# Sorted v re-tiled through DRAM and x^T by crossbar DMA, for the last two batches, with loads and attention alternating

## The chip, the cores and the metric

One core of a Trainium2 chip. The time is the device time of one execution in microseconds (us), each kernel run several times. "Span" is the length of one profiled execution; it leaves out about 2 us that the device time has on top. In the profiles PE is TensorE, PEld its weight loads, DVE VectorE, ACT ScalarE, POOL GpSimd and SP SyncE (SPq its queue); PSUM is the memory that matmuls write to, and a copy out of it frees a slot.

## The reference, cut to what matters

```python
# q, k, v: (4, 8, 768, 64); sort_net: (4, 8, 8, 8); w_in: (512, 2048); w_out: (2048, 512)
P = sinkhorn(sort_net)                                   # five rounds of exp and normalizing
k_sorted = einsum('bhij,bhjcd->bhicd', P, k_blocks)      # 8 blocks of 96 rows, mixed by P
v_sorted = einsum('bhij,bhjcd->bhicd', P, v_blocks)
attn = softmax(q_block @ k_sorted_block.T / 8)           # inside each block of 96 only
x = (attn @ v_sorted_block)  ->  (3072 tokens, 512)
out = relu(x @ w_in)**2 @ w_out                          # the FFN
```

## The kernel before

Everything on TensorE is bf16. Tokens are cut in 8 FFN groups of 384, two to a batch. A group is 28 chunks: 16 up-projections of 4 matmuls (128x384) and 12 quarter down-projections of 4 matmuls (128x512). The attention of a batch is worked off in 4 pairs of heads and slipped between the chunks of earlier groups. A small planner in the Python code simulates the engines with given costs and so fixes the order of all instructions; the chip then runs that order, whatever the true durations are.

For one head pair the sort of v, the transposes that re-tile sorted v by block, and the transposes of x are all on TensorE, each with a copy out of PSUM:

```python
def s_sort(u, t, due=0, ...):            # t = 1: k, t = 2: v
    for a in range(NA):                  # 6
        for h in range(2):               # weights of 64 columns: 12 narrow matmuls
            nc.tensor.matmul(out=tp[64 * h:64 * (h + 1), a, :],
                lhsT=src[:, 2 * u.hp + h, D * a:D * (a + 1)],
                rhs=w_all[:, H * u.b + 2 * u.hp + h, ...], start=True, stop=True)
    ...                                  # cast to ksT or vsT
def s_vt(u, due=0):                      # 8 transposes of vsT, then a copy to vs
    ...
def s_xt(u, due=0):                      # 8 transposes of ao, then a copy to xT
    ...
for b, (c0, c1) in enumerate(((n_up, 2 * n_up), (2 * n_up, 4 * n_up), (4 * n_up, 6 * n_up)), 1):
    lay(b, (0, 1), c0, c1)               # batch 1 beside group 1; 2 beside 2, 3; 3 beside 4, 5
```

PSUM is full: one slot `p1` (q, v and x transposes), two slots `p2` (sorts, scores, attention times v), three for the FFN.

The softmax here doesn't subtract the row's maximum and nothing guards it: scores larger than these inputs give would overflow.

## Time and profile before

| | before |
|---|---|
| time, median of 3 | 241.82 us |
| span of the profiled run | 238.9 us |
| TensorE busy | 96% |
| one FFN group alone | 20.76 us |

TensorE sets the time. The readings are in the prediction below. **The attention of batches 2 and 3 on TensorE's path** is the stretch from the end of batch 1's last FFN chunk to the first up-projection of group 6, less the four FFN groups in it (4 x 20.76 = 83.04 us). Before, the stretch is 193.28 - 85.61 = 107.67 us, so this attention costs 24.6 us.

### The profile page before, as it was taken

How to read it: one execution, taken by the hardware profiler on the slowest of the kernel's cores; microseconds unless marked ns; L12 is line 12 of the kernel's file. 1: busy time of each engine (PE TensorE's matmuls, PEld its weight loads, DVE VectorE, ACT ScalarE, POOL GpSimd, SP SyncE). 2: the span in 40 equal slices, each digit the busy share in tenths (PEclk: the TensorE clock that was granted, in tenths of full speed). 3: DMA queues.
4: the chain of work that ended last, by engine and by line, in shares of the span. 5: the costliest groups of instructions: out<-in, count | busy, mean ns of one | idle time of the engine just before them, and what ended most of it. 6: DMA issues, size and time to landing. Idle time of an engine off the chain costs nothing.

```text
span 238.9 us, 5867 instructions
## 1 busy us (share of the span) xinstructions
PE 230.5 (96%) x2485; PEld 138.1 (58%) x2501; DVE 121.4 (51%) x322; ACT 123.0 (51%) x256; POOL 27.0 (11%) x41
## 2 busy tenths in 40 slices
PE   7899999999999999999999999999999999999993
PEld 2777665556675556655665456655665456446541
DVE  6677777327785347744676037643666025105400
ACT  4365675237885247724674147723674147227510
POOL 8843221500006000000000000000000000000000
PEclk9999999999999999999999999999999999999999
DMA  6999999999405990011100120011100120011012
GB/s 81 193 204 207 206 207 206 201 241 222 76 3 68 220 238 9 3 44 47 45 3 0 44 91 0 3 44 47 44 3 1 47 88 1 19 72 44 0 44 88
DMA packets 20489, 20.30 MB, mean 85 GB/s; under 512 B 1008, under 2 KB 17392, under 8 KB 20464
## 3 DMA queue, kind: packets, MB, share of 16 engines
q0 software_dynamic: 16960, 13.63, 36.8%
q1 hardware_dynamic: 3504, 6.30, 7.2%
q8 instruction: 19, 0.31, 0.5%
q14 instruction: 6, 0.05, 0.1%
HBM read 27.27 MB, written 6.29 MB: 140 GB/s over the span
## 4 chain that ended last, share of the span: by engine, by line
PE 91%; DVE 4%; ACT 2%; issue 1%; POOL 0%; POOLq 0%
PE hp L562 35%; PE op L590 34%; PE tp L403 5%; PE vbp L472 3%; PE qtp L361 3%; PE oup L499 3%; PE scp L439 3%; PE xtp L531 3%; ACT qT L166 1%; DVE p_sb L266 1%; PE fill L283 0%; DVE vs L168 0%; ACT h L570 0%; DVE rs L265 0%; POOL qb L212 0%
## 5 line engine op out<-in xcount | busy, mean ns | idle before, releaser
L562 PE MATMUL hp<-xT,w_in_bf 128*128 128x384 bf16 x512 | 92.8, 326 | 0.0
L590 PE MATMUL op<-w_out_bf,h 128*128 128x512 bf16 x368 | 86.2, 379 | 1.0 <-issue 0.3
L570 ACT ACTIVATE h<-hp 128x384 bf16<-128x384 f32 x128 | 62.3, 494 | 26.1 <-PE hp L562 25.4
L573 DVE TENSOR_TENSOR h<-h 128x384 bf16<-128x384 bf16 x128 | 43.9, 354 | 37.2 <-ACT h L570 36.7
L562 PEld LDWEIGHTS <-w_in_bf 128*128 128x128 bf16 x512 | 46.4, 98 | 28.1
L590 PEld LDWEIGHTS <-h 128*128 128x128 bf16 x384 | 36.1, 98 | 39.7
L166 ACT COPY ob<-op 128x512 f32<-128x512 f32 x24 | 14.1, 586 | 57.5 <-PE op L590 57.5
L455 ACT ACTIVATE et<-scp 96x384 bf16<-96x384 f32 x64 | 26.4, 490 | 6.7 <-PE scp L439 6.7
L509 DVE TENSOR_TENSOR ao<-oup,rec 96x512 bf16<-96x512 f32 x32 | 22.0, 687 | 1.1
L168 DVE COPY vs<-vbp 96x1024 bf16<-96x1024 bf16 (+1 forms) x20 | 11.6, 580 | 19.5 <-PE vbp L472 19.4
L168 DVE COPY qT<-qtp 128x768 bf16<-128x768 bf16 (+1 forms) x15 | 7.3, 489 | 18.9 <-PE qtp L361 18.4
L166 ACT CAST ksT<-tp 128x768 bf16<-128x768 f32 (+1 forms) x17 | 11.7, 686 | 9.9 <-PE tp L403 9.6
L168 DVE COPY xT<-xtp 128x768 bf16<-128x768 bf16 (+1 forms) x16 | 7.9, 496 | 13.3 <-PE xtp L531 12.8
L283 PE MATMUL fill<-ones 128*128 128x128 bf16 (+1 forms) x108 | 12.0, 255 | 1.5 <-DVE ones L185 1.5
L499 PEld LDWEIGHTS <-et 96*128 96x128 bf16 x256 | 10.7, 98 | 3.1 <-ACT h L570 0.6
L168 DVE CAST vsT<-tp 128x768 bf16<-128x768 f32 (+1 forms) x14 | 11.8, 840 | 0.8
L499 PE MATMUL oup<-vs,et 96*128 96x65 bf16 x256 | 11.6, 193 | 0.2 <-DVE vs L168 0.2
L361 PEld LDWEIGHTS <-qb 128*64 128x64 bf16 (+1 forms) x240 | 6.9, 109 | 7.1 <-issue 5.8
L508 DVE RECIPROCAL rec<-oup 96x8 f32<-96x8 f32 x32 | 6.4, 199 | 8.3 <-PE oup L499 8.1
L472 PE MATMUL vbp<-ident,vsT 128*128 128x128 bf16 x128 | 10.5, 219 | 0.0
L212 POOL DMA_DIRECT2D qb<-in_q_dram x8 | 6.0, 747 | 39.1 <-PE qtp L361 33.3
L361 PE MATMUL qtp<-ident,qb 128*64 128x128 bf16 (+1 forms) x240 | 9.3, 212 | 0.8 <-DVE qT L168 0.4
(48 smaller groups left out, 130.5 us busy)
## 6 DMA issues: line engine op xcount, KB each, us to landing
out_dram<-ob SPq DMA_DIRECT2D x24, 256.0 KB, 2.0
qb<-in_q_dram POOLq DMA_DIRECT2D x8, 384.0 KB, 12.4
kb<-in_k_dram POOLq DMA_DIRECT2D x6, 384.0 KB, 15.1
vb<-in_v_dram POOLq DMA_DIRECT2D x6, 384.0 KB, 16.3
w_in_bf<-in_moe_w_in_dram POOLq DMA_DIRECT2D x4, 512.0 KB, 13.2
w_out_bf<-in_moe_w_out_dram POOLq DMA_DIRECT2D x4, 512.0 KB, 19.3
kb<-in_k_dram POOLq DMA_DIRECT2D x4, 192.0 KB, 6.1
vb<-in_v_dram POOLq DMA_DIRECT2D x4, 192.0 KB, 6.4
```

What stands on the lines that cost most here:

```text
L166: nc.scalar.copy(out=out, in_=in_)
L168: nc.vector.tensor_copy(out=out, in_=in_)
L283: nc.tensor.matmul(out=tiles["fill"][:, 0:w], lhsT=ones[:, 0:128], rhs=ones[:, 0:w], start=True, stop=True)
L361: nc.tensor.transpose(out=t["p"][64 * h:64 * (h + 1), a, :], in_=qb[p0:p1, 2 * hp + h, D * a:D * (a + 1)], identity=ident[p0:p1, p0:p1])
L455: nc.scalar.activation(out=et[:, h, 0:HS].rearrange("p (n c a) -> p n c a", c=C0, a=NA), in_=st["p"][0:96, h, 0:HS].rearrange("p (n a c) - ...
L472: nc.tensor.transpose(out=vbp[:, n, :], in_=u.vsT[:, i // NQ, BLK * (i % NQ):BLK * (i % NQ) + 128], identity=ident)
L499: nc.tensor.matmul(out=oup[:, h, 66 * n:66 * n + D + 1], lhsT=et_r[u.et[hf]][:, h, BLK * n:BLK * n + 128], rhs=u.vs[:, NQ * hf + n, h, 0:D ...
L509: nc.vector.tensor_tensor(out=u.ao[:, n0:n0 + NQ, :, :].rearrange("p n e d -> p e n d"), in0=ov[:, :, :, 0:D], in1=rec[:, :, :, None].to_b ...
L562: nc.tensor.matmul(out=t["hp", nt][:, 0:HS], lhsT=w_in_bf[:, kc, 128 * nt:128 * (nt + 1)], rhs=xT[:, kc, t0:t0 + HS], start=(kc == 0), sto ...
L570: nc.scalar.activation(out=t["h1", nt], in_=t["hp", nt][:, 0:HS], func=AF.Relu)
L573: nc.vector.tensor_tensor(out=t["h2"][:, nt, :], in0=t["h1", nt], in1=t["h1", nt], op=ALU.mult)
L590: nc.tensor.matmul(out=t["op", mt], lhsT=t["h2"][:, nt, 128 * mt:128 * (mt + 1)], rhs=w_out_bf[:, nt, :], start=(nt == 0), stop=(nt == NT ...
```

## The change

Its intent: take work off TensorE for batches 2 and 3. v is sorted un-transposed, by two wide matmuls per pair, written to DRAM and read back in the block layout. x is transposed by crossbar DMA from SyncE's queue. SyncE's order is now fixed by the plan too. Attention of batch 2 moves to FFN group 3 alone, of batch 3 to group 5 alone; the loads of a batch are planned after the transposes of the previous one, with v first of the three.

```diff
+    v_way = nc.dram_tensor("v_way", (B, 2, 128, NA, HP * 66), BF16, kind="Internal").ap()
+    def s_vn(b, g, due):                      # half a batch: two head pairs
+        for hp in (2 * g, 2 * g + 1):
+                for h in range(2):
+                    nc.tensor.matmul(out=st["p"][:, h, 0:NA * D],
+                        lhsT=w_all[:, H * b + 2 * hp + h, :, :].rearrange("p i c -> p (i c)"),
+                        rhs=qkv[b][2][:, 2 * hp + h, :], start=True, stop=True)
...
+        wr = plan.add("SP", 0.1, write, evs)
+        there = plan.add("WAY", 2.3, lambda e: None, [wr])
+        rd = plan.add("SP", 0.1, read, [there] + oldw)
+        back = plan.add("WAY", 2.6, lambda e: None, [rd])
...
     def s_xt(u, due=0):
+        if u.b > 1:
+            def turn(e):
+                nc.sync.dma_start_transpose(
+                    out=xT[:, u.hp, S * u.b:S * (u.b + 1)].rearrange("p (n q) -> p n q", q=BLK),
+                    in_=u.ao.rearrange("p n e d -> p (n e d)"))
+            sp = plan.add("SP", 1.25, turn, u.norms)
+            op = plan.add("WAY", 2.2, lambda e: None, [sp])
...
+            if b > 1 and hp % 2 == 0:
+                todo.append((c0 + 0.6 * (hp // 2), len(todo), v_first, b))
+            if b > 1:
+                c = c0 + 1.5 + gap * hp        # gap = (c1 - c0 - 13) / (HP - 1)
+                todo.append((c, len(todo), open_, b))      # scores at c + 1.8, av at c + 6.2
...
-    ... ((n_up, 2 * n_up), (2 * n_up, 4 * n_up), (4 * n_up, 6 * n_up))
+    ... ((n_up, 2 * n_up), (3 * n_up, 4 * n_up), (5 * n_up, 6 * n_up))
```

More of the change, by code (lines that the diff above doesn't have):

```diff
@@ L43 @@
 class Plan:
-    TAIL = {"PE": 0.0, "ACT": 0.09, "DVE": 0.06, "POOL": 0.0, "DMA": 0.0, "SP": 0.0}
+    TAIL = {"PE": 0.0, "ACT": 0.09, "DVE": 0.06, "POOL": 0.0, "DMA": 0.0, "SP": 0.0, "WAY": 0.0}
     HOP = 0.06
@@ L150 @@
     ctx.enter_context(tc.manual_schedule(engines={
-        mybir.EngineType.PE, mybir.EngineType.DVE, mybir.EngineType.Activation}))
+        mybir.EngineType.PE, mybir.EngineType.DVE, mybir.EngineType.Activation,
+        mybir.EngineType.SP}))
     plan = Plan()
+    rvn, rvb = Ring(2), Ring(3)
     r1, r2, rf, rh1, rh2, rob = Ring(1), Ring(2), Ring(3), Ring(3), Ring(2), Ring(3)
@@ L188 @@
     for n in range(3):
-        for r, name in ((ksT_r, "ksT"), (vsT_r, "vsT")):
-            sT = const.tile([128, 2, HS + 32], BF16, name=f"{name}{n}")
+        for r, name, hs in ((ksT_r, "ksT", 2), (vsT_r, "vsT", 2)):
+            sT = const.tile([128, hs, HS + 32], BF16, name=f"{name}{n}")
             nc.vector.memset(sT[:, :, HS:HS + 32], 0.0)
@@ L195 @@
         vs_r.append(vs)
+    vn_r, vb_r = [], []
+    for n in range(2):
+        vn = const.tile([128, NA, HP, 66], BF16, name=f"vn{n}")
+        nc.vector.memset(vn[:, :, :, D:66], 1.0)
+        vn_r.append(vn)
+    for n in range(3):
+        vb_r.append(const.tile([96, NB, HP, 66], BF16, name=f"vblk{n}"))
+    v_way = nc.dram_tensor("v_way", (B, 2, 128, NA, HP * 66), BF16, kind="Internal").ap()
     for n in range(4):
@@ L227, in load @@
         dma((b, t, h0, p.start), 1.57 * n / H * (p.stop - p.start) / 128, dst_src,
-            readers[b - 2] if b > 1 else [])
+            readers[b - 2] + [x_done[b - 1, x, 0] for x in range(HP)] if b > 1 else [])
     def load_w_in(g):
@@ L248 @@
     for g in range(2):
-        for t in (1, 2, 0):
+        for t in (2, 1, 0):
             load(1, t, HP * g, HP)
@@ L429, in s_sc @@
         u.exps = {}
-        u.et, last = {}, []
+        u.et = {}
         for hf in u.halves:
@@ L450, in s_sc @@
             rqT.use(qTs[u.b, u.hp], pe)
-            last.append(pe)
+            rks.use(u.n, pe)
             u.exps[hf] = []
@@ L461, in s_sc @@
                 u.exps[hf].append(op)
-        u.sc_pe = last
     def s_vt(u, due=0):
@@ L484, in s_vt, with mm, ev, write @@
         r1.use(s1, pe, u.vs_op)
-        rks.use(u.n, pe, *u.sc_pe)
+        rks.use(u.n, pe)
+    v_blk = {}
+    def s_vn(b, g, due):
+        m, oldm = rvn.take()
+        evs = []
+        for hp in (2 * g, 2 * g + 1):
+            st = {}
+            def mm(e, hp=hp, st=st):
+                st["p"] = ps2.tile([128, 2, 512], FP32, tag="p2", name="vnp")
+                for h in range(2):
+                    nc.tensor.matmul(
+                        out=st["p"][:, h, 0:NA * D],
+                        lhsT=w_all[:, H * b + 2 * hp + h, :, :].rearrange("p i c -> p (i c)"),
+                        rhs=qkv[b][2][:, 2 * hp + h, :],
+                        start=True, stop=True)
+            def ev(e, hp=hp, st=st):
+                h0 = 2 * (hp % 2)
+                copy(e, vn_r[m][:, :, h0:h0 + 2, 0:D],
+                     st["p"][:, :, 0:NA * D].rearrange("p e (a d) -> p a e d", d=D))
+            s2, old = r2.take()
+            h0 = H * b + 2 * hp
+            pe = plan.add("PE", 0.34, mm, [landed[b, 2, HP * g, 0], built[h0], built[h0 + 1]]
+                          + old, due)
+            readers[b].append(pe)
+            op = plan.add(AD, cost_f(2 * NA * D), ev, [pe] + oldm)
+            r2.use(s2, pe, op)
+            evs.append(op)
+        def write(e):
+            nc.sync.dma_start(out=v_way[b, g], in_=vn_r[m].rearrange("p a h x -> p a (h x)"))
+        w, oldw = rvb.take()
+        def read(e):
+            nc.sync.dma_start(
+                out=vb_r[w].rearrange("p i h x -> p i (h x)"),
+                in_=v_way[b, g].rearrange("(i c) a x -> (c a) i x", c=C0))
+        wr = plan.add("SP", 0.1, write, evs)
+        there = plan.add("WAY", 2.3, lambda e: None, [wr])
+        rd = plan.add("SP", 0.1, read, [there] + oldw)
+        back = plan.add("WAY", 2.6, lambda e: None, [rd])
+        rvn.use(m, *evs, there)
+        rvb.use(w, back)
+        v_blk[b, g] = w, back
     def s_av(u, due=0):
         nao, olda = rao.take()
+        if u.b > 1:
+            w, u.vs_op = v_blk[u.b, u.hp // 2]
         u.norms = []
@@ L501, in mm @@
                             lhsT=et_r[u.et[hf]][:, h, BLK * n:BLK * n + 128],
-                            rhs=u.vs[:, NQ * hf + n, h, 0:D + 1],
+                            rhs=(u.vs[:, NQ * hf + n, h, 0:D + 1] if u.b < 2 else
+                                 vb_r[w][:, NQ * hf + n, 2 * (u.hp % 2) + h, 0:D + 1]),
                             start=True, stop=True)
@@ L520, in s_av @@
             ret.use(u.et[hf], pe)
-            rks.use(u.n, pe)
+            if u.b < 2:
+                rks.use(u.n, pe)
+            else:
+                rvb.use(w, pe)
             u.norms.append(op)
@@ L525, in s_xt @@
     def s_xt(u, due=0):
+        if u.b > 1:
+            def turn(e):
[4 more added lines that the diff above has]
+            op = plan.add("WAY", 2.2, lambda e: None, [sp])
+            rao.use(u.nao, op)
+            for hf in u.halves:
+                x_done[u.b, u.hp, hf] = op
+            return
         st = {}
@@ L648, in lay @@
     def lay(b, halves, c0, c1):
-        step = (c1 - c0) / (HP + 0.9)
+        step, gap = (c1 - c0) / (HP + 0.9), (c1 - c0 - 13) / (HP - 1)
         for hp in range(HP):
@@ L656, in open_, with v_first @@
                 u.q_op = s_q(b, hp, C0 * u.i0, C0 * (u.i0 + u.ni), due)
-                if b > 0:
+                if b == 1:
                     build_w(H * b + 2 * hp, 2, pt, kops[b - 1, hp])
                 u.k_op = kops[b, hp] = s_sort(u, 1, due)
-                u.v_op = s_sort(u, 2, due)
+                if b < 2:
+                    u.v_op = s_sort(u, 2, due)
+            if b > 1 and hp % 2 == 0:
+                def v_first(due, b=b, g=hp // 2):
+                    for x in (2 * g, 2 * g + 1):
+                        build_w(H * b + 2 * x, 2, pt, kops[b - 1, x])
+                    s_vn(b, g, due)
+                todo.append((c0 + 0.6 * (hp // 2), len(todo), v_first, b))
+            if b > 1:
+                c = c0 + 1.5 + gap * hp
+                todo.append((c, len(todo), open_, b))
+                todo.append((c + 1.8, len(todo), lambda due, box=box: s_sc(box["u"], due), b))
+                todo.append((c + 6.2, len(todo), lambda due, box=box: s_av(box["u"], due), b))
+                todo.append((c + 6.4, len(todo), lambda due, box=box: s_xt(box["u"], due), b))
+                continue
             for f, s in ((0.0, open_),
@@ L669 @@
     lay(0, (1,), 0, n_up)
-    for b, (c0, c1) in enumerate(((n_up, 2 * n_up), (2 * n_up, 4 * n_up), (4 * n_up, 6 * n_up)), 1):
+    for b, (c0, c1) in enumerate(((n_up, 2 * n_up), (3 * n_up, 4 * n_up), (5 * n_up, 6 * n_up)), 1):
         lay(b, (0, 1), c0, c1)
@@ L675 @@
             for g in range(2):
-                for t in (1, 2, 0):
+                for t in (2, 1, 0):
                     load(b, t, HP * g, HP)
```

## The prediction

> **What bounds the kernel now.** I read the page first, then the chain of waits, the TensorE timeline, and a table of stretches. The page says which engine sets the time:
>
> ```profile
> span 238.9 us, 5867 instructions
> ...
> PE 230.5 (96%) x2485; PEld 138.1 (58%) x2501; DVE 121.4 (51%) x322; ACT 123.0 (51%) x256; POOL 27.0 (11%) x41
> ...
> PE 91%; DVE 4%; ACT 2%; issue 1%; POOL 0%; POOLq 0%
> ```
>
> The chain of work that ended last lies 91% on TensorE; VectorE and ScalarE are half idle. Busy TensorE need not be TensorE at its pace, so I check that in the timeline (start, duration, what), here around one head pair of batch 2:
>
> ```profile
> 119.20 0.53 PE L361 MATMUL qtp<-ident,qb 128*64 128x128 bf16 x12
> 119.56 0.50 PE L403 MATMUL tp<-w_all,kb 128*64 128x128 bf16 x12
> 119.89 0.50 PE L403 MATMUL tp<-w_all,vb 128*64 128x128 bf16 x12
> 120.33 1.47 PE L562 MATMUL hp<-xT,w_in_bf 128*128 128x384 bf16 x8
> 121.64 0.51 PE L531 MATMUL xtp<-ident,ao 96*128 96x96 bf16 x8
> 121.98 1.47 PE L562 MATMUL hp<-xT,w_in_bf 128*128 128x384 bf16 x8
> 123.38 0.51 PE L439 MATMUL scp<-qT,ksT 64*128 64x96 bf16 x16
> 123.82 0.82 PE L562 MATMUL hp<-xT,w_in_bf 128*128 128x384 bf16 x4
> 124.48 0.61 PE L472 MATMUL vbp<-ident,vsT 128*128 128x128 bf16 x8
> 124.93 2.11 PE L562 MATMUL hp<-xT,w_in_bf 128*128 128x384 bf16 x12
> 126.88 0.67 PE L499 MATMUL oup<-vs,et 96*128 96x65 bf16 x16
> 127.39 1.46 PE L562 MATMUL hp<-xT,w_in_bf 128*128 128x384 bf16 x8
> ```
>
> The true cost of a burst is its start to the next start, not its duration, because bursts overlap at the ends. 8 up-projection matmuls take 121.64 - 120.33 = 1.31 us (164 ns each), 12 take 126.88 - 124.93 = 1.95 us. No line shows an idle time before it. So TensorE streams without gaps, and any TensorE work removed here shortens the time, as long as nothing new makes it wait.
>
> The stretches (length, busy time and count by engine, clock, DMA share, GB/s) are batch 1's attention beside one FFN group, batch 2's beside two, batch 3's beside two, and FFN alone:
>
> ```profile
> 51.60:85.60 34.00, 33.61 (x446) 20.97 (x448) 21.11 (x48) 21.05 (x43) 4.46 (x6) 1.00 0.78 131
> 85.60:139.50 53.90, 53.58 (x559) 32.05 (x562) 28.97 (x68) 28.09 (x58) 0.00 (x0) 1.00 0.16 45
> 139.50:193.30 53.80, 53.48 (x558) 32.15 (x562) 27.58 (x64) 28.06 (x58) 0.00 (x0) 1.00 0.09 31
> 193.30:224.90 31.60, 31.49 (x178) 17.43 (x179) 11.11 (x31) 17.83 (x36) 0.00 (x0) 1.00 0.09 34
> ```
>
> One FFN group alone runs from 193.28 to 214.04, 20.76 us. So the attention of batches 2 and 3 costs 53.9 - 2 x 20.76 = 12.4 us each, and that of batch 1, squeezed into one group, 34.0 - 20.76 = 13.2 us. The same work costs 0.9 us more when squeezed; this matters below. The clock is full everywhere and DMA is nearly idle from 90 us on.
>
> **What the Trainium skill says.** (1) "TensorE: Matmul & The Clock Gate", section "Back-to-back issue gap": N/2.4 + 2.5 ns warm, so 162.5 ns at N = 384. The trace agrees (60 up-projections in 9.76 us, 163 ns). (2) "VectorE: DVE Perf Modes", section "The three transpose paths": 390 ns for a 128x128 transpose on TensorE, 1309 ns by the DMA crossbar. In this stream 8 TensorE transposes cost 0.34 us, 43 ns each, so the isolated figure overstates what their removal saves; the measurement decides. (3) "DMA: Bandwidth & Descriptors", section "Anatomy of one DMA": about 2.0 us fixed plus bytes/436 GB/s, the fixed part being mostly the receipt. By it a 256 KB store would take 2.6 us; this trace has 2.0:
>
> ```profile
> out_dram<-ob SPq DMA_DIRECT2D x24, 256.0 KB, 2.0
> ```
>
> (4) The same page, section "Latency and other measured facts": a DMA transpose moves 261 GB/s in the poor case. No DMA transpose has run here yet.
>
> **The change part by part, for batches 2 and 3 (8 head pairs).**
>
> Removed from TensorE per pair: the v sort (12 matmuls of 64 columns' weights). In the timeline the first sort costs 0.33 us (119.56 to 119.89) and the second 0.44, but 0.1 us of that is the change back to full-width weights, which the k sort inherits. I take 0.33. The 8 transposes of v: 124.48 to 124.93, 0.45. The 8 transposes of x: 121.64 to 121.98, 0.34. Sum 1.12 us.
>
> Added to TensorE per pair: v is sorted un-transposed by two matmuls of N = 384, with the block weights stationary: 2 x 163 ns = 0.33 us. Net 0.79 us per pair; 8 pairs give **6.4 us**. That is the ceiling, 2.6% of 241.82.
>
> Removed from VectorE/ScalarE per pair: the vsT cast (0.95 us for the 768-wide form on VectorE), the vs copy (0.69), the xT copy (0.56), 2.2 us. Added: one 768-wide cast, 0.80 on ScalarE as for ksT or 0.95. Net relief of about 1.3 us per pair. These engines don't bound, so worth nothing directly, but it shortens the waits in the squeezed windows.
>
> Added on the DMA side, per half batch: a write of 128 x 6 x 264 bf16 = 405,504 bytes to DRAM and a read back in 528-byte rows; per pair one crossbar transpose of 96 x 1024 bf16 = 196,608 bytes. The write I estimate at 2.3 us: the 2.0 us store above plus 143,000 more bytes at the page's 436 GB/s. The code's own schedule assumes 2.3 for the write, 2.6 for the read, and 1.25 us issue plus 2.2 us flight for a transpose; it is an assumption, not a measurement. The bandwidth part of a transpose is about 0.75 us by the page's 261 GB/s (estimate), so 3.45 us in all is plausible. DMA capacity is no issue: about 3.2 MB over two windows where DMA is nearly idle.
>
> Moved: batch 2's attention goes from the two FFN groups 2 and 3 into group 3 alone, batch 3's into group 5. A load is planned after the previous batch's transposes. But the planned dependency only orders the program; the buffer still comes free when batch b-2's last reader is done, and the transfers that would wait are on a queue of their own. I expect the loads where they are now (issued at 41 to 47 and 73 to 78 us), with no collision and no cost.
>
> **What of the 6.4 us is given back.** (a) Squeezing: it costs batch 1 0.9 us. Batches 2 and 3 will have less for ScalarE and VectorE to do, and p1, the one-slot PSUM buffer that q, v and x shared, serves q alone. I take 0.5 us per batch, 1.0 in all. (b) The end of each window. The last pair's attention-times-v is due at chunk 22 of 28; 6 down-projection chunks of 4 x 216 ns, 5.2 us, remain, and its own 0.5 us. Against it: half of it 0.26, then two norms of 0.20 + 0.69 us each with handovers (about 2.0), then 3.45 us for the transpose, 5.7 us in all. These are equal: nothing is in reserve except that only the fourth contraction step of the next up-projection needs this pair (0.49 us). Each microsecond by which the real transpose exceeds the assumption is paid by TensorE, twice. I take 0.3 us per batch, 0.6 in all. (c) The start of each window. The first pair's attention-times-v is due at chunk 7: 7 x 0.65 us plus four v sorts (1.3), two openings (1.4) and the scores (0.5) is about 7.8 us after the window opens. v is back after two sorts (0.65), casts on shared engines (about 1.5), 2.3, 2.6 and handovers, 7.2 us. Slack about half a microsecond; I take 0.2 us per batch, 0.4 in all.
>
> Sum: 6.4 - 1.0 - 0.6 - 0.4 = 4.4 us saved; 241.8 - 4.4 = 237.4. Since (a) may vanish, because the freed VectorE and p1 are what caused the waits in batch 1, I shade it to **237.2 us**, 1.9% less.
>
> **The rivals.** *The whole gain arrives*: all DMA latency is hidden, squeezing is free. For it: VectorE and ScalarE half idle, DMA idle after 90 us, constants that look fitted to the latencies. Against it: batch 1's 0.9 us. Time 235.4. *The DMA wait replaces the transpose*: crossbar transposes or the DRAM round trip take 2 us longer than planned, and since TensorE's order is fixed it stands still at the start of FFN groups 4 and 6 and at the first attention-times-v. For it: no slack in (b), and stores share the in-order SP queue with transposes and with a read that waits for its write. Against it: the squeeze of the schedule around exactly these latencies. It costs 2 us at two to four places: 239.5 to 243. *An engine becomes the bound*: batch 1's window has 21 us busy on ScalarE and on VectorE in 34 us; the new windows of about 30 us have less work, so no. *Loads collide with transposes*: slow transposes in batch 2 if batch 3's load really moves; I count on it at 1 in 10, 1 to 3 us.
>
> **Range and chances.** The low end is 6.4 us saved with nothing given back, 235.4. The high end is the planned latencies missed by about 1 us at the window ends with the squeeze at batch 1's cost, 239.4. The line of 2% is 237.0, a saving of 4.8 us, so the loss has to stay under 1.6 us; my sum of losses is 2.0, with some hope in (a). Faster 0.43, within 2% 0.53, slower 0.04 (it would take over 10 us of stalls).
>
> **What would show each step.** TensorE bursts: no v sort of 12, no vbp and xtp in batches 2 and 3, instead pairs of 128x384 matmuls at about 163 ns; TensorE busy time about 6 us less. Squeeze: the windows of groups 3 and 5 near 20.8 + 9.1 + 0.5 = 30.4 us, groups 2 and 4 at 20.8. (b): idle of TensorE before the first up-projection of groups 4 and 6, released by a transpose; none if the transpose lands within 3.4 us. (c): idle before the first attention-times-v of a batch, released by the read of v. Loads: issues near 41 and 73 us; if they stand near 86 and 136 I was wrong on the move. A time over 239.4 would mean a transpose or round trip far slower than assumed; one under 235.4, that the bursts removed cost more than their start-to-start times.

## The result, and the profile after

239.36 us (median of 4 runs, 238.96 to 239.49) against 241.74 before in the same rounds; ratio 0.9896, 95% interval 0.9878 to 0.9914. A ratio is the mean time of one kernel's runs over that of the other's of the same rounds, so not quite the ratio of the medians quoted. Executions over 1.5% slower than the fastest of the same kernel are left out of the means. About 1% faster, inside the 2% band, at the upper edge of the predicted range; the saving is 2.4 us where 4.4 was summed up and 6.4 was the ceiling.

The page of the changed kernel, in the lines that answer to those before:

```profile
span 237.0 us, 5484 instructions
...
PE 229.2 (97%) x2293; PEld 130.9 (55%) x2293; DVE 109.0 (46%) x303; ACT 126.3 (53%) x261; POOL 27.0 (11%) x41
...
PE 89%; DMA 4%; DVE 3%; ACT 2%; issue 1%
```

TensorE still sets the end, but DMA now stands in the chain with 4%. The stretches whose lengths give the sum for the attention (window, length, then busy time and count of PE, PEld, DVE, ACT and POOL, granted clock, DMA share, GB/s), first before, then after:

```profile
85.61:193.28 107.67, 107.04 (x1114) 64.19 (x1122) 56.56 (x132) 56.15 (x116) 0.00 (x0) 1.00 0.12 38
```

```profile
86.58:190.76 104.18, 103.80 (x913) 56.55 (x912) 43.99 (x111) 59.45 (x121) 0.00 (x0) 1.00 0.34 85
```

201 recorded matmuls fewer, but only 3.5 us shorter: the attention went from 24.6 to 21.1 us, not to 18.2. TensorE's timeline at the start of batch 3's window shows where the rest is:

```profile
159.24 0.81 PE L510 MATMUL vnp<-vb,w_all 128*128 128x384 bf16 x4
159.88 0.81 PE L641 MATMUL hp<-xT,w_in_bf 128*128 128x384 bf16 x4
160.77 0.81 PE L510 MATMUL vnp<-vb,w_all 128*128 128x384 bf16 x4
161.51 0.53 PE L373 MATMUL qtp<-ident,qb 128*64 128x128 bf16 x12
161.97 0.82 PE L641 MATMUL hp<-xT,w_in_bf 128*128 128x384 bf16 x4
162.72 0.53 PE L415 MATMUL tp<-w_all,kb 128*64 128x128 bf16 x12
163.18 1.47 PE L641 MATMUL hp<-xT,w_in_bf 128*128 128x384 bf16 x8
...
167.23 2.12 PE L641 MATMUL hp<-xT,w_in_bf 128*128 128x384 bf16 x12
169.45 0.67 PE L562 MATMUL oup<-vblk,et 96*128 96x65 bf16 x16
...
171.36 0.72 PE L451 MATMUL scp<-qT,ksT 64*128 64x96 bf16 x16
172.00 0.53 PE L373 MATMUL qtp<-ident,qb 128*64 128x128 bf16 x12
```

Read start to start. The four wide v sorts cost 0.64 us, as predicted. But the four up-projections after them take 0.89 us instead of 0.65: 0.24 us of waiting before the next v sorts. q and k no longer stand together as before; each takes 0.46 us alone between full-width matmuls, against 0.36 and 0.33 inside a block. The 12 up-projections at 167.23 take 2.22 us instead of 1.95: 0.27 us of waiting for v to come back. The scores at 171.36 take 0.64 us. Before, they took 0.44 with an up-projection behind them; here narrow q transposes follow, which would make it about 0.35 (see below), so some 0.3 us is waiting.

**The price of a narrow burst that stands alone.** In the timeline before, 8 up-projections ahead of x transposes took 1.31 us, ahead of scores 1.40; the k sort took 0.33 us with the v sort behind it, the v sort 0.44 with an up-projection behind it. So going in and out of narrow bursts (q, k, v sorts and scores) costs about 0.1 us at each edge, 0.19 per block. Batches 2 and 3 had 16 such blocks before (q, k and v together, and the scores, for 8 pairs) and have 21 after: 1.0 us. The price is read from four lines of one timeline; no run changes the edges alone.

Two things outside that stretch also moved. The warm-up of TensorE, 14 matmuls at the start, took 4.54 us in the trace before and 6.07 after:

```profile
1.53 4.54 PE L283 MATMUL fill<-ones 128*128 128x512 bf16 x14 [1.53 <-DVE ones L185]
```

```profile
1.53 6.07 PE L295 MATMUL fill<-ones 128*128 128x512 bf16 x14 [1.53 <-DVE ones L187]
```

And SyncE's closing semaphore waits (count, durations, then first and last start) stretch over 3.4 us instead of 2.9, before and after:

```profile
L716 SPq EVENT_SEMAPHORE  x11: 17/28/28, 236.0 to 238.9; - x11
```

```profile
L810 SPq EVENT_SEMAPHORE  x11: 17/28/28, 233.5 to 236.9; - x11
```

The spans add up: 238.9 - 3.5 (attention) + 1.0 (start) + 0.6 (end) = 237.0.

### The profile page after: what moved, and what is told of

Same layout as the page of the kernel before. It is cut to its first block, busy times and chain, and to the rows that moved or that the text cites. A ratio compares the mean times of both kernels' runs of the same rounds, so it can differ in the third digit from the quotient of the medians.

```text
span 237.0 us, 5484 instructions
## 1 busy us (share of the span) xinstructions
PE 229.2 (97%) x2293; PEld 130.9 (55%) x2293; DVE 109.0 (46%) x303; ACT 126.3 (53%) x261; POOL 27.0 (11%) x41
## 2 busy tenths in 40 slices
DMA packets 30600, 25.10 MB, mean 106 GB/s; under 512 B 7536, under 2 KB 26992, under 8 KB 30576
## 4 chain that ended last, share of the span: by engine, by line
PE 89%; DMA 4%; DVE 3%; ACT 2%; issue 1%
PE op L669 35%; PE hp L641 33%; PE tp L415 4%; PE scp L451 3%; PE oup L562 3%; PE qtp L373 3%; PE fill L295 3%; PE vbp L483 2%; DMA v_way<-vn 2%; DMA vblk<-v_way 2%; PE xtp L610 1%; PE vnp L510 1%; ACT qT L168 1%; DVE ao L573 1%; DVE vs L170 0%
## 5 line engine op out<-in xcount | busy, mean ns | idle before, releaser
L669 PE MATMUL op<-w_out_bf,h 128*128 128x512 bf16 x384 | 87.2, 379 | 0.0
L295 PE MATMUL fill<-ones 128*128 128x128 bf16 (+1 forms) x108 | 13.5, 272 | 1.5 <-DVE ones L187 1.5
L168 ACT CAST ksT<-tp 128x768 bf16<-128x768 f32 (+1 forms) x16 | 10.9, 680 | 4.2 <-PE tp L415 3.9
L170 DVE CAST vn<-vnp 128x768 bf16<-128x768 f32 x4 | 3.8, 958 | 19.6 <-PE vnp L510 19.6
L170 DVE COPY qT<-qtp 128x768 bf16<-128x768 bf16 (+1 forms) x13 | 6.2, 480 | 10.7 <-PE qtp L373 10.4
L451 PEld LDWEIGHTS <-ksT 64*128 64x128 bf16 x256 | 6.2, 94 | 7.7 <-issue 2.0
L295 PEld LDWEIGHTS <-ones 128*128 128x128 bf16 x108 | 7.3, 104 | 5.2 <-issue 3.3
L451 PE MATMUL scp<-qT,ksT 64*128 64x96 bf16 x256 | 10.0, 205 | 0.1
L415 PE MATMUL tp<-w_all,kb 128*64 128x128 bf16 (+1 forms) x240 | 9.1, 212 | 0.2 <-ACT ksT L168 0.2
```

The costliest lines, as they stand in the source:

```text
L168: nc.scalar.copy(out=out, in_=in_)
L295: nc.tensor.matmul(out=tiles["fill"][:, 0:w], lhsT=ones[:, 0:128], rhs=ones[:, 0:w], start=True, stop=True)
L415: nc.tensor.matmul(out=tp[64 * h:64 * (h + 1), a, :], lhsT=src[:, 2 * u.hp + h, D * a:D * (a + 1)], rhs=w_all[:, H * u.b + 2 * u.hp + h, u ...
L451: nc.tensor.matmul(out=scp[:, h, BLK * n:BLK * (n + 1)], lhsT=u.ksT[64 * h:64 * (h + 1), hf, BLK * n:BLK * n + 128], rhs=qT[64 * h:64 * (h ...
L669: nc.tensor.matmul(out=t["op", mt], lhsT=t["h2"][:, nt, 128 * mt:128 * (mt + 1)], rhs=w_out_bf[:, nt, :], start=(nt == 0), stop=(nt == NT ...
```

## The experiments

Theory A: the ceiling is right, and the gain was given back to the squeezed order (more narrow blocks, waits at the opening of the windows). Rival B: the DMA latencies of the new paths hold TensorE up wherever they stand. Twelve runs were made, eleven new kernels and the changed one again, all correct, each against the kernel before in the same rounds. Kernels of different rounds are compared through these ratios. The last column is from one trace each; the changed kernel's two traces differ by 0.15 us in it.

| kernel | median us | ratio | attention of batches 2 and 3, us |
|---|---|---|---|
| before | 241.26 to 241.74 | 1 | 24.6 |
| changed | 239.36; again 239.18 | 0.9896; 0.9911 | 21.1; 21.3 |
| squeeze_only | 242.92 | 1.0059 | 26.2 |
| v_only | 238.51 | 0.9875 | 21.9 |
| x_only | 240.39 | 0.9950 | 23.3 |
| spread | 237.81 | 0.9850 | 20.1 |
| spread_merged | 241.13 | 0.9984 | 23.6 |
| merged | 238.67 | 0.9880 | 21.0 |
| early_v | 237.53 | 0.9840 | 20.0 |
| early_v_x_pe | 237.74 | 0.9853 | 21.0 |
| best | 235.88 | 0.9769 | 18.4 |
| best_noglue | 236.01 | 0.9775 | 18.4 |
| best_x_pe | 237.60 | 0.9852 | 21.0 |

### The squeeze undone, and the squeeze alone

`spread`, against the changed kernel:

```diff
-    ... (3 * n_up, 4 * n_up), (5 * n_up, 6 * n_up)
+    ... (2 * n_up, 4 * n_up), (4 * n_up, 6 * n_up)
-            readers[b - 2] + [x_done[b - 1, x, 0] for x in range(HP)] if b > 1 else [])
+            readers[b - 2] if b > 1 else [])
```

> The changed kernel with one thing undone: the attention of batches 2 and 3 is laid over two FFN groups each again, as before the change, and the planned dependency of the loads on the transposes is dropped (in the trace of the changed kernel it never delayed a load: they were issued at 41 and 74 us). Theory A, the squeeze into one FFN group gave the gain back (more bursts of narrow-weight matmuls standing alone among full-width ones, at about 0.19 us each, and small waits, together about 1.4 us per batch): the whole 6.4 us on TensorE comes through less a tail that is 0.6 us longer, so about 236.2 us, within 0.8; attention of batch 2 costs about 9.2 us over its two FFN groups instead of 10.4. Rival B, the round trip through DRAM and the transposes hold TensorE up wherever they stand: 238.5 to 240. Rival C, the loads had to be kept from the transposes: slower than the changed kernel.

`squeeze_only`, against the kernel before: only the first of these two edits, the other way round.

> The kernel before with one thing changed: batches 2 and 3 are squeezed into FFN groups 3 and 5, nothing goes by DMA. Theory A: each batch then costs as batch 1 does, 13.2 us instead of 12.4 or a little more, so 243.3 to 244.5 us. Rival B: squeezing is free, 241.5 to 242.

Spread is faster than the changed kernel (0.9850 against 0.9896, and their 95% intervals do not overlap), so squeezing did cost: 1.1 to 1.2 us of attention, 0.5 to 0.6 per batch. But 237.8 is not the 236.2 of theory A; it lies above A's range and below B's. Its attention costs 20.1 us, not 18.4: something else is left, partly a wait of 0.33 us for v. Squeezing alone costs 26.2 - 24.6 = 1.6 us (0.8 per batch) and 0.6% of time, a little under what theory A expected; rival B's "squeezing is free" falls. (It has 20 narrow blocks against 16, which at 0.19 us is about half of the 1.6.) What rival C forecast, a slower kernel, did not come; its mechanism was not tested, for no transpose ran beside a load in any of these traces.

### One part of the change alone

`v_only` drops the DMA branch of `s_xt`; `x_only` keeps it, and v goes by `s_sort` and `s_vt` again. Both are squeezed.

> The changed kernel with x transposed on TensorE again, v still by way of DRAM, still squeezed. Theory A: the removed x transposes were worth 8 x 0.34 = 2.8 us, so the time is 2.8 us above the changed kernel, about 242.1 us, perhaps less by half a microsecond where the squeeze's waits absorb some of it. Rival B with the x transposes at fault: under 240.5. Rival D, bursts are worth less than start to start: under 241.

> The changed kernel with v sorted and transposed on TensorE again, x still by crossbar DMA, still squeezed. Theory A: the v part was worth 8 x (0.33 + 0.45 - 0.33) = 3.6 us, so about 242.9 us. Rival B with the DRAM round trip at fault: under 240.5.

Against `squeeze_only` (26.2) x_only saves 2.9 us of attention where 2.7 was counted (8 x 0.34), and v_only 4.3 where 3.6 was. (Both also have the changed kernel's way of laying out the steps of a batch, which squeeze_only has not.) Together they save 26.2 - 21.1 = 5.1, not 6.4 and not 7.2. So each part delivers alone, and the two get in each other's way.

Both expectations of theory A missed by far, and both times fell where rival B had put them. x_only took 240.39 us where 242.9 was expected: beside x by DMA, v by way of DRAM was worth 23.25 - 21.14 = 2.1 us of attention, not 3.6. v_only took 238.51 where 242.1 was expected: with x back on TensorE the kernel was no slower than the changed one (that it was faster is not shown, since the intervals of the ratios, 0.9857 to 0.9892 and 0.9878 to 0.9914, overlap). In attention x by DMA still gained 0.6 to 0.7 us; the end of the program took it back, as the next group shows.

The transfers differ too, once each is looked up in the traces by itself. In the changed kernel batch 3's first write of v took 4.3 us to land (4.1 in the repeat), in v_only 2.4; three of its eight transposes took 4.2 to 4.5 us and a fourth 3.4, while none in x_only took over 3.3. No load was in flight then. Why these transfers are slower where both ways are in use is open.

### What repeats, and which waits they are

`after_again` is the changed kernel unaltered.

> The changed kernel unaltered, as the comparison for this group and for a second reading of the two things that differ between runs or programs: the warm-up of TensorE (14 matmuls of 512 columns took 4.54 us in the trace before and 6.07 in the changed one) and the end (0.48 us between two of the closing semaphore waits). If the warm-up is a matter of chance it is another number between 4.5 and 6.1 here; if it belongs to the program it is about 6.07 again. The gap at the end is expected again. Time 239.0 to 239.6 us.

The warm-up of the same program was this time:

```profile
1.53 4.61 PE L295 MATMUL fill<-ones 128*128 128x512 bf16 x14 [1.53 <-DVE ones L187]
```

So it is chance, and the 1.0 us at the start of the first comparison doesn't belong to the change. (6.07 us is 434 ns a matmul; the trace's clock column shows 1.00 there all the same, so what slows it is not shown here.) The stretch at the end came again (232.6 to 236.0). In all kernels that have both new paths TensorE's last matmul ends 4.5 to 4.7 us before the span does; in all others 3.9 to 4.0. And device time less span is 2.5 us in the changed kernel against 2.1 before, though only 2.2 in early_v and spread. About 0.9 us of fixed cost in the changed kernel is thus outside any of the steps argued over. What causes it no run has shown.

`early_v` sorts v in the group without attention: `c0 - 8 + 4 * (hp // 2)` in place of `c0 + 0.6 * (hp // 2)`.

> The changed kernel with the sorting of v moved 8 and 4 chunks ahead, into the FFN group that has no attention, so that v has long been back when the first attention-times-v runs. Theory A: what goes is the wait for v of 0.27 us in batch 3 and the two waits of 0.24 us between v sorts, so about 0.7 us, 238.6 us. Rival B, the round trip is what the gain was lost to: 2 us or more, 237.4 or less.

1.1 to 1.3 us of attention went, more than the 0.7 expected and less than rival B's 2: not only the wait for v and the two waits between v sorts, but also most of those inside the score bursts, which share the two `p2` slots (the weight loads of the scores wait there for the VectorE step, `ao<-oup,rec`, that empties the slot). The time fell by 1.65 us, to 237.53, nearer to B's forecast than to A's; about 0.35 of that is the smaller device time less span. What came up instead was one wait at the start of FFN group 4:

```profile
PE hp L641 <- DMA xT<-ao: 0.6, 1, 0.6
```

`merged` ties q to k and the score halves to each other, in the planner (`pe.glue`: the first is not issued until both can be).

> The changed kernel with the q transposes tied to the k sort, and the second half of the scores tied to the first, so that narrow-weight bursts no longer stand alone: 16 such blocks in batches 2 and 3 at most instead of 21. Theory A (each block costs 0.19 us at its two edges): 5 x 0.19 = 1.0 us less, and the waits inside the score bursts (0.6 us) gone: about 238.0 us; if tying makes the chain of a batch longer than its window, an idle time of TensorE before FFN groups 4 and 6 eats it. Rival, the edges cost nothing that the order can change: no difference.

A miss: 238.67 against 239.18 in the same rounds, with overlapping intervals. The blocks fell from 21 to 16 as meant, but attention only from 21.1 (21.3 in the repeat) to 21.0: waits for a free PSUM slot (0.5 us) and for a transpose (0.6 us) took the place of the edges. In this squeezed window the edges could not be had for nothing.

`spread_merged` adds to spread the tying, a later attention-times-v and a later second half of v.

> Everything that theory A asks for: attention over two FFN groups, q tied to k and the score halves to each other, attention-times-v two chunks later, the second half of v sorted 18 chunks after the first. Against the spread version (237.8 us): 18 blocks become 16 (0.4 us), the wait for v of 0.33 us and the waits around the v sorts (0.9 us) go; about 236.3 us. Rival: at the level of the spread version.

A clear miss, and the most telling one. TensorE's waits and SyncE's (total, times, longest):

```profile
PE oup L571 <- DMA vblk<-v_way: 3.3, 1, 3.3
```

```profile
SPq L545 <- DMA v_way<-vn: 8.0, 4, 4.6
```

The write was issued at 87.6 us, while batch 3's load (issued 73.7 to 78 us) was still landing; its last part landed at 91.0. The write took 5.0 us to land and the read, issued only at 92.6, another 4.8. In the same kernel batch 3's first write and read, with no load in flight, took 2.4 and 3.7, and nothing waited. (The read of batch 2 was issued when the load was in; why it too took 1.1 us more is not shown.) In batch 2 TensorE stood still:

```profile
97.46 0.67 PE L571 MATMUL oup<-vblk,et 96*128 96x65 bf16 x16 [3.31 <-DMA vblk<-v_way]
97.97 5.09 PE L650 MATMUL hp<-xT,w_in_bf 128*128 128x384 bf16 x20
102.99 0.53 PE L380 MATMUL qtp<-ident,qb 128*64 128x128 bf16 x12
```

The 20 up-projections after the wait took 5.02 us where 3.25 is normal: the granted clock had dropped, to 0.59 from 98 to 99 us, 0.50 until 101 and 0.70 until 102.

```profile
99.00:100.00 1.00, 1.00 (x5) 0.46 (x4) 1.00 (x3) 0.49 (x1) 0.00 (x0) 0.50 0.00 0
```

The Trainium skill ("TensorE: Matmul & The Clock Gate", "HAM oscillation — how this bites in real kernels") warns of this for idle gaps of some 3.4 us; here 3.3 us was enough, in one case. The wait and the clock together, 3.3 + 1.8 us, are nearly the whole distance to the best kernel below (23.6 against 18.4).

That the load slowed the write is argued from its company: three stores of 256 KB beside the same load took 4.8 to 7.0 us to land, against a median of 2.1. Spread's first write, issued at 88.0, took 4.8 too. It got off with 0.33 us because TensorE reached attention-times-v 10.0 us after the first v sort began, and 8.2 us after it here. So alternating loads and attention does matter, but for the round trip of v: in the changed kernel batch 2's attention starts at 107 us, after the load has landed. A load is not the only thing that slows a write, though, as the 4.3 us above show.

### What the runs point to

`best` keeps v away from batch 3's load and gives both batches room:

```diff
-    ... (3 * n_up, 4 * n_up), (5 * n_up, 6 * n_up)
+    ... (3 * n_up - 10, 4 * n_up), (5 * n_up - 22, 6 * n_up)
-                todo.append((c0 + 0.6 * (hp // 2), len(todo), v_first, b))
+                todo.append((c0 - 8 + 4 * (hp // 2), len(todo), v_first, b))
```

with the load's planned wait dropped as in spread, 14 for 13 in the gap, and the tying of `merged`; `best_noglue` is without the tying. `early_v_x_pe` and `best_x_pe` are early_v and best with x transposed on TensorE.

> The layout that the runs point to: v sorted 8 and 4 chunks ahead of the attention but after batch 3's load has landed (92 us), attention of batch 2 over the last 38 chunks before it is needed and of batch 3 over the last 50, q tied to k and the score halves to each other. Theory A: attention of batches 2 and 3 costs 24.6 - 6.4 = 18.2 us on TensorE, plus 0.3; early-v has 20.0. So 1.5 us below early-v, 236.0 us. Rival: tying turns the edges into waits again, 237 or more.

> The same layout without tying q to k or the score halves. Theory A: 2 to 4 narrow blocks more at 0.19 us, so 0.4 to 0.8 us above the tied one, 236.6 us. Rival, the order inside a batch doesn't matter: equal.

> The early-v version with x transposed on TensorE again: what the crossbar transposes are worth once the waits for v are gone. Theory A: 8 x 0.34 = 2.8 us of TensorE work come back, 0.6 us of waiting for a transpose at the start of FFN group 4 and 0.5 us at the end of the program go, so 1.5 to 1.8 us slower than early-v: 239.0 us, attention of batches 2 and 3 near 21.8 us. Rival E, the transposes by DMA are worth nothing (the v-only version at 238.5 us was no slower than the changed kernel at 239.2): 237.5 to 238.0 us.

> The best layout with x transposed on TensorE again. In the squeezed layout the crossbar transposes took 1.0 us off TensorE's path instead of 2.8 (20.0 against 21.0 us for the attention of two batches), because the schedule put four narrow blocks more and a wait for a transpose in their place. Theory A: with room in the layout they are worth all of it: attention 18.4 + 2.8 = 21.1 us, time 235.9 + 2.8 - 0.5 (the end of the program) = 238.2 us. Rival E, they are worth about 1 us whatever the layout: 236.4 us.

The stretch in best:

```profile
86.23:187.63 101.40, 100.60 (x904) 56.59 (x912) 44.30 (x112) 57.87 (x120) 0.00 (x0) 1.00 0.35 88
```

101.40 - 83.04 = 18.4 us: 6.3 of the 6.4 us of the ceiling have arrived. By its time best is 2.3% below the kernel before and beats both. Rival B falls with it as far as it said "wherever they stand": the same transfers hold nothing up here. Tying made no difference here (16 blocks either way, and no release by a DMA in TensorE's waits of either), so that expectation was wrong. The crossbar transposes are worth 21.0 - 18.4 = 2.6 us of attention in this layout, as theory A says, and 0.85% of time. In the squeezed early_v they were worth 1.0 us of attention, and the times (237.53 and 237.74) differ by less than the noise: there theory A's 239.0 missed and rival E's forecast came true. Over both layouts rival E falls: what they are worth hangs on the layout. Early_v has 20 narrow blocks and a wait of 0.6 us for a transpose where early_v_x_pe has 16 and none.

## Why the prediction was right or wrong

**The ceiling, 6.4 us: right** (8 x 0.79 is nearer 6.3). Best shows 6.3, and best_x_pe puts 2.6 of it on x, where 8 x 0.34 = 2.7 was counted. Start-to-start costs are what removal saves, and rival "bursts are worth less" falls.

**The bound: right.** TensorE sets the time before and after, and no other engine became it. One sign failed: TensorE's busy time was to fall by about 6 us and fell by 3.2 in the stretch (107.04 to 103.80); TensorE counts as busy in nearly all of the stretch either way, so that figure only follows the stretch's length. **The loads: right.** They were issued at 41.7 to 45.4 and 74.4 to 78.4 us, as foretold, since the planned dependency orders the program only. I didn't foresee that it lands only at 91 us, where a round trip of v that starts early runs into it. The 3.2 MB of DMA traffic left out the transposes; the page shows 25.10 - 20.30 = 4.8 MB more, which cost nothing by its amount.

**(a) Squeezing, taken as 0.5 us per batch: between right and too small.** squeeze_only measured 0.8, close to batch 1's 0.9; spread, which undoes it in the changed kernel, 0.5 to 0.6. The hope that (a) would vanish, because freed VectorE and `p1` had caused batch 1's waits, did not come true: what held TensorE up were the `p2` slots and the narrow edges. The windows of groups 3 and 5 took 31.1 and 31.5 us instead of 30.4; groups 2 and 4 took 20.8 as foretold.

**(b) The window ends, 0.3 us per batch: too large for the changed kernel, and partly by luck.** There was no wait at the start of groups 4 and 6. Issue was 1.22 us, and a transpose landed a median of 3.2 us after its issue began, against the planned 1.25 + 2.2. But batch 2's last one took 4.4 and landed at 138.81, after group 4 had begun at 138.47 and 0.15 us before the fourth contraction step (0.49 us later) would have waited for it. In early_v and merged that transpose took 4.6 us, and TensorE waited 0.6. The last line below is the transpose, the first two the write and the read (KB each, us to landing):

```profile
v_way<-vn SPq DMA_DIRECT2D x4, 396.0 KB, 3.0
vblk<-v_way SPq DMA_DIRECT2D x4, 396.0 KB, 4.1
xT<-ao SPq DMA_TRANSPOSE x8, 3.2
```

**(c) The window starts, 0.2 us per batch: the term that failed most.** early_v puts it at 1.1 to 1.3 us in all. The wait for v itself was 0.27 us once. The rest was what I had not listed: four v sorts in a row through two `p2` slots (0.24 us twice), and score halves waiting for a slot behind them. The round trip was also longer than summed, a median of 3.0 + 4.1 instead of 2.3 + 2.6: the first one of batch 2 took 2.4 + 3.9 and cost no wait, that of batch 3 took 4.3 + 4.2.

**Not in the sum at all:** the longer end and the larger device time less span, 0.9 us.

Summed anew: 6.4 - 1.6 (squeeze alone) - 0 - 1.2 - 0.9 = 2.7 us, or 3.2 with the 1.1 us that spread gives for the squeeze, against 2.4 measured. These runs are not strictly additive, so a few tenths of agreement is as much as can be asked.

**The rivals.** "The DMA wait replaces the transpose" wasn't the mechanism of the changed kernel, but it is real: spread_merged shows it with 3.3 us. The mean of 237.2 leaned to the optimistic side, and shading it down from 237.4 was the wrong way. That the range held by a hair (239.36 of 239.4) is luck in part: its high end was reasoned from transposes at the window ends, which cost nothing, while the losses came from the window starts and the end of the program.

What stays open: the cause of the longer end, why single writes and transposes are slower when both ways are in use, and whether a crossbar transpose beside a running load is slow, since none ran so.

## What to carry to other kernels

Work taken off the bounding engine is worth its start-to-start time, but only if the order that the change brings with it is no worse: count how often the engine switches kinds of burst and which buffer slots the moved work now shares, not just the work removed. When two parts come in one change, run each alone; here each paid by itself, and x by DMA added only 0.6 to 0.7 us beside the other until the layout was loosened. Place a latency-bound round trip where no bulk load is in flight, and give it more slack than its latency measured on an idle queue.

## What the Trainium skill lacked or had wrong

- "TensorE: Matmul & The Clock Gate", "Back-to-back issue gap", has no price for alternating between full-width weights and weights of 64 columns or rows: about 0.1 us at each edge here, 0.19 us per block. No other page that I found has a time for it either, and no run shows its cause.
- The same page, "Part 1: The HAM clock gate", says the warm-up varies between runs because its window runs free. That it varies the runs confirm; what it lacks is a size for comparisons: 14 matmuls took 4.61 and 6.07 us in two executions of one program, so single executions can't settle a difference under about 1.5 us.
- "VectorE: DVE Perf Modes", "The three transpose paths": its 390 against 1309 ns says little for a stream. Eight TensorE transposes cost 0.34 us in sequence; one DMA transpose of 96x1024 landed after a median of 3.2 us (2.8 to 4.5) and held SyncE's queue for 1.22 us, which the page doesn't give.
- "DMA: Bandwidth & Descriptors", "Anatomy of one DMA", fits its formula to DMAs issued by GpSimd; the stores and the round trip here are issued by SyncE, for which the page has no such fit, so the prediction's use of it was out of place. The store of 256 KB landed after 2.0 us, where the formula would give 2.6. The four writes of 405,504 bytes landed after 2.4, 2.5, 4.3 and 3.4 us, the read back in rows of 528 bytes after a median of 4.1, and the write beside a bulk load after 5.0.
- No page that I found has the closing semaphore waits of a program: they stretched over 3.4 us instead of 2.9 in the changed kernel.
